# 48 drains on TensorE behind the loop of a decode kernel, and a load of x that waits for SyncE

## The chip, the core and the metric

The kernel runs on one core of one Trainium2 chip. The metric is the device time of one execution in microseconds; the span is the time from the first to the last instruction in the profile of one execution, and is a little shorter than the execution's own time.

## What is computed

One decode step (one new token for each of four sequences): a layer norm, then attention over the last 4096 positions of a cache and a SwiGLU feed-forward network side by side, both added to the input.

```python
# B=4, D=512, Hq=32, Hkv=8, Sk=16384, Dh=128, W=4096, F=1792, bfloat16
xn = layernorm(x)
q = xn @ wq                                    # [4, 32 heads, 128]
k, v = k_cache[:, :, Sk - W:], v_cache[:, :, Sk - W:]     # each kv head serves 4 q heads
p = softmax(q @ k.T * Dh ** -0.5)
attn = (p @ v) @ wo
ffn = (silu(xn @ w_gate) * (xn @ w_up)) @ w_down
out = x + attn + ffn
```

## The kernel before

The kernel is written engine by engine, with semaphores between the engines set by hand. The order of each engine's work is the order in the text; there is no scheduler.

**The work and its loop.** The 4 x 8 pairs of sequence and kv head are taken two at a time: 16 steps `d`, each with a K block and a V block of 2 MB (two sequences x 4096 positions x 128). K and V have two buffers each in SBUF. TensorE runs a loop of 8 rounds (line 425) with two steps `b` in each. A step waits for its K block, then takes, in this order: `transposes(0)` (the first half of K, against an identity matrix, into four PSUM banks), `max_rows` (the transposed row maxima of the step before), `pv(b, 1)` (the second half of probabilities times V of an earlier step), `scores(0)`, `shift` (subtracts the row maximum by a small matrix product into the score bank), `transposes(1)`, `pv(1 - b, 0)`, and `scores(1)`. VectorE copies the transposed K out of PSUM (L294), reduces the row maxima (L299), and divides by the denominators (L310 to L314). ScalarE does the exponentials (L263).

**SyncE** issues nearly all loads from one queue, in this order: WQ (4 MB, L231), K(0), K(1) (L217), the gate and up weights WG and WU (L234, L235), V(0) (L221), then in turn K(d) and V(d - 1), each behind a wait until TensorE has released the buffer: `s_tr` for K, `s_pv` for V. Behind those come WD (L240), the last V block in two halves (L225), which wait for the sixteenth increment of `s_pv`, and WO in four pieces (L229). `s_pv` is incremented by `pv(b, 1)`, which stands inside the loop.

**ScalarE** issues the load of x (4 KB, L252) as its first instruction. VectorE waits for x, reduces its sum (L272), and ScalarE and VectorE go in turn through the layer norm (L254, L256, L274, L258, L276, L260). TensorE transposes the result (L359), VectorE copies it to `XnT` (L279), and TensorE then waits for WQ and forms the 32 products of the Q projection.

**Behind the loop** TensorE has, in order: the last `max_rows`, which waits for VectorE's reduction `s_rm`, `pv(0, 1)`, the last `shift`, the gate and up products, the residual x, the two halves of the last `pv`, the down products (L354 with `wd_sb`), four transposes of the attention output (L462), four products that put the heads in order, and 64 products with WO, in pieces of 32, 20, 8 and 4, each behind the wait for its piece of WO:

```python
            for c in range(NO):
                if c in WO_CUTS:
                    eng.wait_ge(d_wo[WO_CUTS.index(c)], 16)
                for n in range(2):
                    last = mm(ps_acc[64 * n:64 * n + B, 0:256], OP[:, c, :], WO[:, c, 256 * n:256 * n + 256])
```

All of down products, residual and WO products add up in one PSUM bank (`ps_acc`), which VectorE copies out at the end (L349), and SyncE and ScalarE store half each.

## Time and profile before

| | |
|---|---|
| median of 3 runs | 197.38 us (197.1 to 198.93) |
| the profiled execution | 196.99 us |
| its span | 195.2 us |
| mean granted clock of TensorE | 0.991 |
| busy: TensorE, VectorE, ScalarE, GpSimd | 160.9, 114.8, 16.6, 10.3 us |
| moved by DMA | 81.10 MB, mean 416 GB/s over the span |
| share of the chain that ended last | DMA 63%, TensorE 32% |

A row of the timeline has start, duration, engine, line, operation, output and inputs, the number of merged instructions, and in brackets the idle time before it with what ended it. `PEld` is TensorE's weight load, `SPq`, `ACTq` and `PEldq` are sequencers: instructions that the engine itself does not execute, such as the issue of a DMA, a drain or a branch. A row of the windows view has a stretch, its length, the busy time of each engine with its instructions, the granted clock, the share of the DMA engines and GB/s. Line 354 is the helper `mm`, through which most products go; there the names of the tiles tell them apart.

### The profile page before, as it was taken

The page shows a single profiled execution, that of the slowest core. Times are in us where ns is not written, and L with a number is a line of the kernel's source. Part 1 is how long each engine was busy: PE and PEld are TensorE (multiplying, and loading weights), DVE is VectorE, ACT ScalarE, POOL GpSimd, SP SyncE. Part 2 cuts the span into 40 slices and gives each one's busy share as a digit, 9 for nine tenths or more (in the row PEclk, how much of TensorE's full clock was granted, in tenths as well). Part 3 has the DMA queues.
Part 4 walks back from the last instruction along what each step waited for, and adds up shares of the span by engine and source line. Part 5 has one row for each costly group of instructions (what it writes and reads, how often), then busy time and mean ns, then how long its engine had stood idle before and what let it go on. Part 6 is the DMA issues. An engine that isn't in the chain of part 4 may idle for free.

```text
span 195.2 us, 7741 instructions
## 1 busy us (share of the span) xinstructions
PE 160.9 (82%) x3458; PEld 139.5 (71%) x3458; DVE 114.8 (59%) x250; ACT 16.6 (9%) x26; POOL 10.3 (5%) x23
## 2 busy tenths in 40 slices
PE   0127999379898989898989898989898989898954
PEld 0113898368887888788878887878787878786742
DVE  1004777337676767676767676767676767675610
ACT  6600101001010101010101010101010101010100
POOL 8930000000000000000000000000000000000000
PEclk9999999879999999999999999999999999999999
DMA  6999999999999999999999999999999999999991
GB/s 216 430 430 433 435 423 428 425 433 433 430 437 430 430 433 430 430 437 430 433 430 433 430 430 433 430 430 430 430 433 430 430 430 433 430 431 417 442 404 64
DMA packets 5934, 81.10 MB, mean 416 GB/s; under 512 B 668, under 2 KB 680, under 8 KB 936
## 3 DMA queue, kind: packets, MB, share of 16 engines
q1 hardware_dynamic: 5912, 81.01, 97.5%
q8 instruction: 5, 0.08, 0.1%
q10 hardware_dynamic: 16, 0.01, 0.0%
q14 instruction: 1, 0.01, 0.0%
HBM read 81.01 MB, written 0.00 MB: 415 GB/s over the span
## 4 chain that ended last, share of the span: by engine, by line
DMA 63%; PE 32%; issue 1%; DVE 1%; SPq 1%; DVEq 0%
DMA kbuf<-in_A_k_cache_dram 48%; PE ps_kt L382 16%; DMA wo_sb<-in_A_wo_dram 9%; PE ps_s L354 8%; DMA wq_sb<-in_A_wq_dram 6%; PE ps_o L354 5%; PE ps_kt L354 2%; PE ps_acc L354 2%; DVE kT L294 1%; SPq L225 1%; DVE kT L282 0%; SPq L229 0%; DVE y_sb L349 0%; DVE qz L285 0%; DVEq L293 0%
## 5 line engine op out<-in xcount | busy, mean ns | idle before, releaser
L294 DVE COPY kT<-ps_kt 128x1024 bf16<-128x1024 bf16 x128 | 79.5, 684 | 25.3 <-PE ps_kt L382 25.3
L382 PE MATMUL ps_kt<-ident,kbuf 128*128 128x128 bf16 x1024 | 62.8, 219 | 10.6 <-DMA kbuf<-in_A_k_cache_dram 10.6
L382 PEld LDWEIGHTS ps_kt<-ident,kbuf 128*128 128x128 bf16 x1024 | 57.3, 98 | 15.8 <-issue 15.7
L354 PE MATMUL ps_o<-p,vbuf 128*128 128x64 bf16 x1120 | 39.0, 194 | 0.0
L354 PEld LDWEIGHTS ps_s<-qz,kT 128*128 128x128 bf16 x1024 | 32.1, 99 | 6.7 <-issue 3.6
L354 PEld LDWEIGHTS ps_o<-p,vbuf 128*128 128x128 bf16 x1120 | 35.8, 99 | 1.1
L354 PE MATMUL ps_s<-qz,kT 128*128 x1024 | 35.3, 193 | 1.2
L299 DVE TENSOR_REDUCE rm<-ps_s 128x8 bf16<-128x512 f32 x17 | 11.8, 692 | 23.5 <-PE ps_s L354 23.5
L263 ACT ACTIVATE p<-ps_s 128x512 bf16<-128x512 f32 x17 | 10.1, 597 | 162.4 <-PE ps_s L354 162.4
L354 PE MATMUL ps_o<-p,ones 128*128 128x128 bf16 (+1 forms) x69 | 6.9, 220 | 4.4 <-DMA vbuf<-in_A_v_cache_dram 3.0
L354 PEld LDWEIGHTS ps_o<-p,ones 128*128 128x128 bf16 x69 | 4.5, 98 | 5.5 <-DMA vbuf<-in_A_v_cache_dram 3.2
L354 PE MATMUL ps_kt<-wq_sb,xnT 128*32 128x512 bf16 x32 | 3.6, 629 | 5.6 <-DMA wq_sb<-in_A_wq_dram 5.6
L354 PE MATMUL ps_s<-dg,ones 8*128 8x512 bf16 x17 | 6.5, 385 | 0.0
L354 PE MATMUL ps_s<-mkc,mkr 2*128 2x512 bf16 x17 | 6.5, 385 | 0.0
L359 PE MATMUL ps_acc<-i,xn 4*128 4x4 f32 x4 | 0.6, 254 | 7.1 <-ACT xn L260 7.1
L354 PEld LDWEIGHTS ps_kt<-wq_sb,xnT 128*32 128x32 bf16 x32 | 1.2, 137 | 7.2 <-issue 7.2
L282 DVE STREAM_TRANSPOSE kT<-ps_kt 128x512 f32<-128x512 f32 x2 | 1.4, 716 | 8.3 <-PE ps_kt L354 8.3
L354 PE MATMUL ps_acc<-wo_sb,oP 128*4 128x256 bf16 x64 | 4.1, 272 | 1.8 <-DMA wo_sb<-in_A_wo_dram 1.8
L359 PEld LDWEIGHTS ps_acc<-i,xn 4*128 4x128 f32 x4 | 0.6, 207 | 7.1 <-issue 7.1
L310 DVE TENSOR_REDUCE den<-ps_o 128x8 f32<-128x128 f32 x18 | 4.9, 274 | 1.0 <-PE ps_o L354 1.0
L207 POOL MEMSET vbuf<- 128x6144 f32 x1 | 5.2, 5222 | 0.0
L354 PEld LDWEIGHTS ps_acc<-wo_sb,oP 128*4 128x4 bf16 x64 | 2.5, 84 | 3.3 <-DMA wo_sb<-in_A_wo_dram 1.9
(65 smaller groups left out, 48.0 us busy)
## 6 DMA issues: line engine op xcount, KB each, us to landing
kbuf<-in_A_k_cache_dram SPq DMA_DIRECT2D x16, 2048.0 KB, 12.6
vbuf<-in_A_v_cache_dram SPq DMA_DIRECT2D x15, 2048.0 KB, 11.3
wq_sb<-in_A_wq_dram SPq DMA_DIRECT2D x1, 4096.0 KB, 12.4
vbuf<-in_A_v_cache_dram SPq DMA_DIRECT2D x2, 1024.0 KB, 9.2
wo_sb<-in_A_wo_dram SPq DMA_DIRECT2D x1, 2048.0 KB, 14.4
wg_sb<-in_B_w_gate_dram SPq DMA_DIRECT2D x1, 1792.0 KB, 25.8
wu_sb<-in_B_w_up_dram SPq DMA_DIRECT2D x1, 1792.0 KB, 29.4
wd_sb<-in_B_w_down_dram SPq DMA_DIRECT2D x1, 1792.0 KB, 15.0
```

What stands on the lines that cost most here:

```text
L207: eng.memset(VB[:, HKN:].bitcast(FP32), 0.0)
L225: eng.dma_start(VB[:, a:a + HKN], kv_ap(A_v_cache, d)[:, :, h * HKN:(h + 1) * HKN]).then_inc(done, 16)
L263: eng.activation(P[:, d % 2 * PS:d % 2 * PS + SN], ps_S[d % 2][:], ACT.Exp, scale=SCALE).then_inc(s_p, 1)
L282: eng.transpose(qT[:, 512 * n:512 * n + 512], ps_kt[n][:])
L294: eng.tensor_copy(KT[:, u * HKN + 1024 * g:u * HKN + 1024 * (g + 1)], kt_ps[g].rearrange("p a b -> p (a b)")).then_inc(s_ev, 1)
L299: eng.tensor_reduce(RM[:], ps_S[bank][:].rearrange("p (t c) -> p c t", c=C), AX.X, ALU.max).then_inc(s_rm, 1)
L310: eng.tensor_reduce(den[:], den_ps.rearrange("p (t c) -> p c t", c=C), AX.X, ALU.add)
L354: return eng.matmul(o, l, r, start=start, stop=stop, skip_group_check=True)
L359: last = eng.transpose(xT_ps[:, c * B:(c + 1) * B], xn[:].rearrange("b (p c) -> b c p", c=NC)[:, c, :], I4[:])
L382: last = eng.transpose(kt_ps[g][:, k, :], KB[:, a:a + 128], ident[:])
```

## The change

Two edits. Behind TensorE's loop, ahead of the last `max_rows`, stand 48 drain instructions, each of which lets the sequencer go on when the engine has finished what it was given. And ScalarE's load of x, the first instruction of that engine, waits for a new semaphore `s_go`, which SyncE increments with a `nop` right behind its issue of K(1).

```diff
+    s_go = sem("s_go")
...
             eng.dma_start(WQ[:], wq_ap).then_inc(d_wq, 16)
             load_k(0)
             load_k(1)
+            eng.nop().then_inc(s_go, 1)
             eng.dma_start(WG[:], wg_ap).then_inc(d_wg, 16)
             eng.dma_start(WU[:], wu_ap).then_inc(d_wu, 16)
...
         @block.scalar
         def _(eng):
+            eng.wait_ge(s_go, 1)
             eng.dma_start(X[:], x_ap).then_inc(d_x, 16)
...
                     scores(1, ev + NG, b, q)
+
+            for _ in range(48):
+                eng.drain()
             max_rows(ND + 1)
             pv(0, 1, ND + 1)
             shift(1, ND + 1)
```

## The prediction

> **What bounds the kernel now.** I read the page's summary first, then the chain that ended last, then the timelines of the two places that are edited (the first 16 us and the last 20 us).

> ```profile
> span 195.2 us, 7741 instructions
> ...
> GB/s 216 430 430 433 435 423 428 425 433 433 430 437 430 430 433 430 430 437 430 433 430 433 430 430 433 430 430 430 430 433 430 430 430 433 430 431 417 442 404 64
> ```

> From the second slice to the last but one the DMA engines move some 430 GB/s without a break: the loads stream through and the compute engines follow. The end of the chain shows what finishes the kernel:

> ```profile
> 171.95 0.54 SPq L225
> ...
> 173.83 16.82 DMA wo_sb<-in_A_wo_dram
> ...
> 190.69 2.23 PE ps_acc L354 x32
> ...
> 192.95 0.43 DVE y_sb L349
> ```

> The last loads (two halves of V, four pieces of WO) are issued from 171.95 on, when the loop's last `pv` is done; both edits leave that step inside the loop. TensorE ends at 192.92, VectorE copies, the store goes out. So a delay of TensorE behind the loop costs nothing until its own chain ends later than the last piece of WO allows. How much room that is decides this case.

> **Edit 1: the 48 drains.** They stand between the last `scores` of the loop and `max_rows(ND + 1)`.

> ```profile
> 176.73 1.06 PE L354 MATMUL ps_s<-qz,kT 128*128 x32
> 177.83 0.69 DVE L299 TENSOR_REDUCE rm<-ps_s 128x8 bf16<-128x512 f32 x1 [1.15 <-PE ps_s L354]
> 178.57 0.22 PE L354 MATMUL ps_acc<-ident,rm 128*8 128x128 bf16 x1 [0.78 <-DVE rm L299]
> ...
> 186.08 0.41 DVE L345 COPY oB<-ps_kt 32x512 bf16<-32x512 bf16 x1 [1.03 <-PE ps_kt L462]
> 186.54 0.22 PEld L354 LDWEIGHTS ps_kt<-oB,rep 32*128 32x128 bf16 x4 [0.68 <-DVE oB L345]
> 186.98 0.44 DVE L347 CAST oP<-ps_kt 128x128 bf16<-128x128 f32 x1 [0.49 <-PE ps_kt L354]
> 187.68 1.91 PE L354 MATMUL ps_acc<-wo_sb,oP 128*4 128x256 bf16 x32 [0.74 <-DMA wo_sb<-in_A_wo_dram]
> 190.69 2.22 PE L354 MATMUL ps_acc<-wo_sb,oP 128*4 128x256 bf16 x32 [1.09 <-DMA wo_sb<-in_A_wo_dram]
> ```

> There are two covers. The first is the 0.78 us in which TensorE waits for the row maxima anyway (177.79 to 178.57). The second is the wait for WO at the end. The 32 first products take 1.91 us, so one costs (1.91 - 0.27)/31 = 0.053 us and all 64 without a wait 63 x 0.053 + 0.27 = 3.6 us. VectorE has `OP` ready at 187.42; a step from VectorE to TensorE takes 0.05 us (186.49 to 186.54). Free of the DMA, TensorE would end at 187.47 + 3.6 = 191.1, and it ends at 192.92: 1.8 us of room. (WO itself is in by 192.5: the last issue at 174.8 and 17.7 us, rows below, so at 191.1 + 1.8 its wait is over too.) Between the two covers nothing absorbs: TensorE is busy all the time, and waits for no load there that a later start could find landed:

> ```profile
> 180.00:182.00 2.00, 2.00 (x37) 0.94 (x36) 1.35 (x5) 0.84 (x2) 0.00 (x0) 1.00 1.08 459
> 182.00:184.00 2.00, 2.00 (x67) 2.00 (x68) 1.49 (x5) 0.01 (x1) 0.00 (x0) 1.00 1.03 430
> ```

> Now the price of one drain behind another, which this trace does not hold. What it holds:

> ```profile
> L491 PEldq DRAIN  x1: 8/8/8, 0.3 to 0.3; - x1
> L425 PEldq ALU_OP  x1: 32/32/32, 177.2 to 177.2; - x1
> L425 PEldq COMPARE_BRANCH  x1: 76/76/76, 177.3 to 177.3; - x1
> 172.31 0.27 DVE L310 TENSOR_REDUCE den<-ps_o 128x8 f32<-128x128 f32 x1
> 172.66 0.20 DVE L312 RECIPROCAL den<-den 128x8 f32<-128x8 f32 x1
> L229 SPq DMA_DIRECT2D wo_sb<-in_A_wo_dram x4: 432/432/601, 173.2 to 174.8; - x4
> 173.18 2.02 SPq L229 DMA_DIRECT2D wo_sb<-in_A_wo_dram  x4
> wo_sb<-in_A_wo_dram SPq DMA_DIRECT2D x1, 256.0 KB, 17.7
> ```

> TensorE's one drain with nothing to wait for executes in 8 ns. An instruction of the sequencer costs more than its execution, though: SyncE's four issues execute in 601 + 3 x 432 = 1897 ns and take 2.02 us, so 41 ns pass between two. On TensorE's own sequencer the loop's addition (32 ns) and its branch start about 0.1 us apart, which leaves some 0.07 us between. VectorE has a drain between its reduction and its reciprocal, and 0.08 us between the end of the one (172.58) and the start of the other. Bounds for one drain in a row: 0.008 + 0.041 = 0.049 us below, 0.1 us above (the spacing of TensorE's pair). I take 0.08 us: TensorE's own pair with the first one's 32 ns replaced by 8 gives 0.076, VectorE's row 0.08. The first drain also waits until the products are done, so the row starts at 177.8.

> 48 x 0.08 = 3.84 us. TensorE restarts at 177.79 + 3.84 + 0.05 = 181.68 in place of 178.57: 3.1 us late. 1.8 us of that vanish in the wait for WO; 1.3 us are exposed. At 0.049 us a drain: 2.35 us, 1.6 us late, all hidden. At 0.1: 4.8 us, 4.1 us late, 2.3 exposed.

> [...]

> **What the idle time does to the clock.** The drains keep the array idle for 3.9 us. The trace has one idle stretch of that kind, 3.03 us in front of 37.50:

> ```profile
> 37.50 0.40 PE L354 MATMUL ps_o<-p,ones 128*128 128x128 bf16 x4 [3.03 <-DMA vbuf<-in_A_v_cache_dram]
> 37.73 1.71 PE L354 MATMUL ps_o<-p,vbuf 128*128 128x64 bf16 x32
> 44.46 1.11 PE L354 MATMUL ps_o<-p,vbuf 128*128 128x64 bf16 x32
> 37.50:39.20 1.70, 1.70 (x35) 1.70 (x36) 0.00 (x0) 0.00 (x0) 0.00 (x0) 0.64 0.99 414
> 39.20:41.00 1.80, 1.79 (x37) 1.70 (x34) 0.00 (x0) 0.00 (x0) 0.00 (x0) 0.50 0.98 419
> 41.00:42.40 1.40, 0.00 (x0) 0.00 (x0) 0.69 (x1) 0.00 (x0) 0.00 (x0) 0.87 1.01 433
> 190.00:192.00 2.00, 1.31 (x22) 0.87 (x24) 0.00 (x0) 0.00 (x0) 0.00 (x0) 1.00 0.53 205
> ```

> The third figure from the end is the granted clock. It falls to a half soon after the wait and is back by 42.4: at a half for 1.7 x 0.72 + 1.8 + 1.4 x 0.26 = 3.4 us. The same 32 products then take 1.71 us in place of 1.11, so 35% of that time is lost where TensorE is the bound. An idle 1.09 us (the last row) left the clock alone. 3.9 us are longer than the 3.03 that made it fall, so I expect it to fall here, right where TensorE has no idle time: up to 3.4 x 0.35 = 1.2 us, and since part of the low stretch can lie in the stall itself, I take 1.1 us. Bounds: 0 and 1.2.

> [...]

> **Edit 2: x waits for SyncE.**

> ```profile
> 0.81 0.56 ACTq L252 DMA_DIRECT2D x_sb<-in_A_x_dram  x1
> 1.27 1.29 SPq L217 DMA_DIRECT2D kbuf<-in_A_k_cache_dram  x2
> 2.27 0.67 DVE L272 TENSOR_REDUCE st_neg<-x_sb 4x1 f32<-4x512 bf16 x1 [2.27 <-DMA x_sb<-in_A_x_dram]
> 7.73 0.17 DVE L279 CAST xnT<-ps_acc 128x16 bf16<-128x16 f32 x1 [1.55 <-PE ps_acc L359]
> 13.30 3.18 PE L354 MATMUL ps_kt<-wq_sb,xnT 128*32 128x512 bf16 x28 [5.61 <-DMA wq_sb<-in_A_wq_dram]
> 21.93 0.55 SPq L221 DMA_DIRECT2D vbuf<-in_A_v_cache_dram  x1
> ```

> The issue of x moves from 0.81 behind SyncE's second K, 2.56: 1.75 us later, and the whole normalisation on ScalarE, VectorE and TensorE (with ScalarE's table loads, which stand behind the waiting load) moves with it. x landed 1.46 us after its issue; the chain from there to `XnT` takes 7.90 - 2.27 = 5.63 us; the Q projection waits for WQ until 13.2. So x may land as late as 7.5 us, 4.9 us after the new issue. From below it lands as fast as before, at 4.0. From above it stands behind all 8 MB already queued: 8.39 MB at 430 GB/s are 19.5 us, so about 21.3. Which is nearer? A packet of code went through while SyncE's queue held far more than that:

> ```profile
> 3.24 0.45 SPq L235 DMA_DIRECT2D wu_sb<-in_B_w_up_dram  x1
> wu_sb<-in_B_w_up_dram SPq DMA_DIRECT2D x1, 1792.0 KB, 29.4
> q8 instruction: 1, 0.02, 5.4%
> ```

> The last row is of the DMA view from 23.8 to 24.9 us, while WU (issued at 3.24, 29.4 us to landing) is not in before 32.6. Another queue's packet takes its turn among SyncE's. x is four rows on ScalarE's own queue, so I expect it by 5 to 7 us: cost nothing, hidden by WQ. Even an x that comes with WQ at 13.2 only moves the projection by 5.6 us and the load of V(0) to 27.5, with the DMA queue busy until 32.6. Without the cover the upper bound decides: the projection 13.6 us late, V(0) issued at 35.5 in place of 21.93, the queue dry from 32.6 for 2.9 us and the start of a transfer (1.5 us by x's row): +4.4 us. SyncE's `nop` costs a few hundredths in front of loads that queue behind 8 MB: nothing.

> **Sum.** The profiled execution took 196.99 us (span 195.2 and 1.8 around it; 0.2% below the median of the runs shown, 197.38). 196.99 + 1.3 (drains past both covers) + 1.1 (clock) + 0 (x) = 199.4 us.

> **Rivals.**
> - Not slower: the drains fit. At 0.049 us a drain or less the delay is at most 1.6 us, ends inside the wait for WO, and the idle 2.4 us are shorter than any that lowered the clock: 197.0. It decides below 2.6/48 = 0.054 us. For it: the 8 ns row. Against it: no row shows TensorE's sequencer passing two instructions of its own in under 0.1 us. Chance 0.20.
> - [...] Chance 0.15.
> - Dear drains: 0.1 us each, 2.3 us exposed, with the low clock's 1.2 at its full: 200.5. For it: TensorE's pair. Chance 0.17.
> - x stands behind the bulk: 196.99 + 4.4 = 201.4, or more with the drains. The code packet speaks against it. Chance 0.05.

> **How the numbers follow.** The forecast, drains past both covers and the clock down, has 0.41; 0.02 is left for faster, for which I know no mechanism (the stream of the DMA is untouched). The range goes from the hidden case, 196.9, to the dear one with a little more, 201.0. One per cent, 2 us, is about what a measurement of this kernel tells from no change. Slower by more: most of the forecast (0.36), the dear drains (0.17), x (0.05) and a little of the clock's rival (0.02): 0.60. Within it: 0.20 + 0.13 + 0.05 = 0.38. Faster 0.02.

> **What the profile after would show.** The first `max_rows` behind the loop at 181.7 (step one; at 180.2 the drains are cheap, at 182.7 dear). The first WO products at about 191 to 192 and all 64 without a wait, VectorE's last copy at about 195.3. PEclk at 5 to 8 in the slices behind 181. The last WO piece still landing at 192.5. x landing before 7.5 and the Q projection still at 13.3, released by WQ. I am wrong if TensorE still waits for WO at the end, if the Q projection starts late and V(0)'s load with it, or if the loop's loads move at all.

## The result and the profile after

The changed kernel takes 199.54 us (median of 6 runs, 199.32 to 200.49) against 197.29 us before (6 runs): a ratio of 1.0107, 95% interval 1.0067 to 1.0147. The forecast was 199.4 us. The profiled execution took 199.32 us with a span of 197.6 us, 2.3 and 2.4 us more than before.

The page's first parts (TensorE's clock and the DMA rate in 40 slices, then the shares of the chain that ended last):

```profile
span 197.6 us, 7790 instructions
...
PEclk9999999859999999999999999999999999999799
...
GB/s 219 432 425 428 431 424 435 433 425 428 401 425 438 428 441 434 431 428 425 428 438 425 441 434 431 428 425 428 438 431 434 434 431 428 420 426 438 422 306 2
...
DMA 49%; PE 40%; issue 4%; DVE 3%; ACT 2%; SPq 1%; DVEq 0%; ACTq 0%
```

The stream of loads is about as full as before until the last two slices. What is new stands at the end: the clock falls to 7 tenths in the third slice from the end, and the last slice (192.7 to 197.6 us) holds no transfers to speak of: the loads are in, and TensorE still works. The timeline behind the loop:

```profile
176.74 1.06 PE L357 MATMUL ps_s<-qz,kT 128*128 x32
177.84 0.69 DVE L302 TENSOR_REDUCE rm<-ps_s 128x8 bf16<-128x512 f32 x1 [1.16 <-PE ps_s L357]
181.22 0.22 PE L357 MATMUL ps_acc<-ident,rm 128*8 128x128 bf16 x1 [3.41 <-issue]
181.37 1.57 PE L357 MATMUL ps_o<-p,vbuf 128*128 128x64 bf16 x32
183.40 1.68 PE L357 MATMUL ps_kt<-wg_sb,xnT 128*32 128x448 bf16 x16
...
191.66 3.66 PE L357 MATMUL ps_acc<-wo_sb,oP 128*4 128x256 bf16 x64 [0.53 <-DVE oP L350]
195.36 0.42 DVE L352 CAST y_sb<-ps_acc 128x256 bf16<-128x256 f32 x1 [3.75 <-PE ps_acc L357]
```

The loop ends where it ended before (its last scores from 176.74, before 176.73). `max_rows` follows at 181.22, 2.65 us late; what it waited for is now "issue", the sequencer. The 64 WO products run in one piece, released by VectorE, and end at 195.32 in place of 192.91. The drains by their line:

```profile
L444 PEldq DRAIN  x48: 8/8/437, 177.4 to 181.2; - x48
```

The first drain waits 437 ns for the products, to 177.85. The others execute in 8 ns (the median of the row), and yet the last one starts at about 181.15, just ahead of `max_rows`: (181.15 - 177.85)/47 = 0.07 us from one to the next, nearly all of it between them. The windows view of the same stretch and of what follows (the third figure from the end is the granted clock):

```profile
178.00:181.20 3.20, 0.00 (x0) 0.00 (x0) 0.53 (x1) 0.00 (x0) 0.00 (x0) 1.00 1.03 438
181.20:183.40 2.20, 2.18 (x35) 1.59 (x35) 0.85 (x4) 0.00 (x0) 0.00 (x0) 0.64 1.03 439
183.40:185.20 1.80, 1.80 (x21) 0.76 (x24) 0.37 (x3) 0.60 (x1) 0.00 (x0) 0.50 1.01 428
185.20:187.20 2.00, 2.00 (x51) 1.39 (x44) 1.69 (x4) 0.25 (x1) 0.00 (x0) 1.00 0.97 408
```

The clock falls to a half within the first microsecond after TensorE restarts: a mean of 0.64 over 2.2 us is 1.6 us at a half and 0.6 us before them (in the same view, 1.00 from 181.2 to 181.8 and 0.50 from 181.8 to 185.2).

The start of the kernel, where x is loaded:

```profile
2.67 0.55 ACTq L255 DMA_DIRECT2D x_sb<-in_A_x_dram  x1
8.30 0.67 DVE L275 TENSOR_REDUCE st_neg<-x_sb 4x1 f32<-4x512 bf16 x1 [8.30 <-DMA x_sb<-in_A_x_dram]
13.99 0.62 PE L357 MATMUL ps_kt<-wq_sb,xnT 128*32 128x512 bf16 x3 [0.27 <-DVE xnT L282]
22.63 0.55 SPq L222 DMA_DIRECT2D vbuf<-in_A_v_cache_dram  x1
```

x lands at 8.3, 5.6 us behind its issue, and no longer in time: the Q projection starts at 13.99, released by `XnT` and not by WQ, and V(0)'s load goes out at 22.63 in place of 21.93. Up to the loop's end nothing is left of this.

### The profile page after: what moved, and what is told of

Read it like the earlier page. It is cut to its first block, busy times and chain, and to the rows that moved or that the text cites. A ratio compares the mean times of both kernels' runs of the same rounds, so it can differ in the third digit from the quotient of the medians.

```text
span 197.6 us, 7790 instructions
## 1 busy us (share of the span) xinstructions
PE 162.8 (82%) x3458; PEld 141.1 (71%) x3458; DVE 115.0 (58%) x250; ACT 16.6 (8%) x26; POOL 10.3 (5%) x23
## 4 chain that ended last, share of the span: by engine, by line
DMA 49%; PE 40%; issue 4%; DVE 3%; ACT 2%; SPq 1%; DVEq 0%; ACTq 0%
DMA kbuf<-in_A_k_cache_dram 46%; PE ps_kt L385 17%; PE ps_s L357 9%; PE ps_o L357 7%; PE ps_acc L357 4%; PE ps_kt L357 3%; DMA x_sb<-in_A_x_dram 3%; DVE kT L297 1%; ACT L261 1%; SPq L218 1%; ACT xn L263 0%; ACT xsq L259 0%; ACT xc L257 0%; DVE kT L285 0%; DVE rm L302 0%
## 5 line engine op out<-in xcount | busy, mean ns | idle before, releaser
L385 PE MATMUL ps_kt<-ident,kbuf 128*128 128x128 bf16 x1024 | 64.2, 222 | 9.8 <-DMA kbuf<-in_A_k_cache_dram 9.8
L385 PEld LDWEIGHTS ps_kt<-ident,kbuf 128*128 128x128 bf16 x1024 | 58.6, 99 | 15.0 <-issue 15.0
L357 PE MATMUL ps_acc<-ident,rm 128*8 128x128 bf16 x17 | 3.7, 219 | 3.4 <-issue 3.4
L307 DVE TENSOR_REDUCE m<-ps_acc 8x1 f32<-8x128 f32 x17 | 4.6, 270 | 2.9 <-PE ps_acc L357 2.9
L275 DVE TENSOR_REDUCE st_neg<-x_sb 4x1 f32<-4x512 bf16 x1 | 0.7, 674 | 8.3 <-DMA x_sb<-in_A_x_dram 8.3
L357 PEld LDWEIGHTS ps_acc<-ident,rm 128*8 128x8 bf16 x17 | 1.4, 82 | 5.2 <-issue 3.5
L317 DVE TENSOR_TENSOR oT<-ps_o,den 128x8 f32 (+1 forms) x18 | 3.0, 167 | 2.9 <-issue 2.7
## 6 DMA issues: line engine op xcount, KB each, us to landing
wg_sb<-in_B_w_gate_dram SPq DMA_DIRECT2D x1, 1792.0 KB, 25.7
wu_sb<-in_B_w_up_dram SPq DMA_DIRECT2D x1, 1792.0 KB, 29.4
wd_sb<-in_B_w_down_dram SPq DMA_DIRECT2D x1, 1792.0 KB, 15.0
```

What stands on the lines that cost most here:

```text
L307: eng.tensor_reduce(m8[:], mt_ps, AX.X, ALU.max)
L317: eng.tensor_tensor(OT[:, 2 * b:2 * b + 2, ds(r * REP, REP)], O_ps.rearrange("p (j h) -> p j h", j=2), den[:].rearrange("p (j h) -> p j h" ...
L357: return eng.matmul(o, l, r, start=start, stop=stop, skip_group_check=True)
L385: last = eng.transpose(kt_ps[g][:, k, :], KB[:, a:a + 128], ident[:])
```

## The experiments

Theory A: of the 2.4 us some 0.9 are drains past both covers, 1.5 are the low clock, and x costs nothing. Rivals: x has a share by way of a WO that lands later (193.3 in this profile, before 192.5), called Theory B below; the covers are smaller than worked out; the clock is not a price of its own.

**Each edit alone.** Drains without the waiting load:

```diff
-            eng.nop().then_inc(s_go, 1)
...
-            eng.wait_ge(s_go, 1)
```

> The 48 drains alone; x is loaded as before. Theory A (drains 0.84 us past both covers, 1.5 us of low clock, x free): +2.3 to 2.5 us over before, the drains 68 ns apart, the first max_rows behind the loop at 181.2, x landed by 2.3. Theory B (the late x gives about 0.8 us of it, by way of WO landing later): +1.5 to 1.7 us, WO in by 192.5 again.

Measured: 1.0141 of before, 1.0117 to 1.0164 (medians 200.25 and 197.21 us). x alone:

```diff
-            for _ in range(48):
-                eng.drain()
```

> The late x alone; no drains. Theory A: the same time as before within 0.3 us; x lands near 8.3, the Q projection starts 0.7 us late at 14.0, V(0)'s load with it, and WO's last piece at 192.5 as before. Theory B: WO's last piece lands near 193.3 and the kernel takes 0.8 us longer.

Measured: 1.0011 of before, 0.9990 to 1.0033. So x is free as far as these runs can tell (0.7 us at most), and the drains are the loss. Theory B falls: the last piece of WO was in by about 192.7 in the profiles of both runs. Why it came later with both edits is not shown; the WO products did not wait for it. But the drains alone cost 2.8 us (2.3 to 3.2), more than Theory A's 2.3 to 2.5. The windows of their profile show why, here cut in lengths of 3.4 us, as long as the clock was down in the changed kernel:

```profile
176.10:179.50 3.40, 1.54 (x49) 1.33 (x45) 1.20 (x2) 0.00 (x0) 0.00 (x0) 1.00 1.01 426
179.50:182.90 3.40, 1.76 (x31) 1.65 (x32) 0.50 (x2) 0.00 (x0) 0.00 (x0) 0.50 1.06 451
182.90:186.30 3.40, 3.40 (x40) 1.38 (x37) 1.31 (x4) 0.78 (x2) 0.00 (x0) 0.50 0.97 411
```

In this execution the clock fell at 179.5, while the drains still ran, and came back at 186.3: 6.8 us of low clock in place of 3.4. `max_rows` starts at 181.14, much as in the changed kernel, but the WO products at 192.36 and not at 191.66:

```profile
181.14 0.27 PE L354 MATMUL ps_acc<-ident,rm 128*8 128x128 bf16 x1 [3.41 <-issue]
192.36 3.66 PE L354 MATMUL ps_acc<-wo_sb,oP 128*4 128x256 bf16 x64 [0.54 <-DVE oP L347]
```

That is 0.7 us, as are the two profiled executions' times apart (199.32 and 200.04). `max_rows` is 2.57 us late here, so the low clock cost 192.36 - (187.47 + 2.57) = 2.3 us. The other runs of the two kernels lie between 199.3 and 200.5 us; whether they differ by the same cause was not profiled.

The profile of x alone shows how near the start came to its limit. Here the expectation missed: x landed at 9.04 in place of 8.3, and V(0)'s load did not follow at 22.6.

```profile
9.04 0.67 DVE L275 TENSOR_REDUCE st_neg<-x_sb 4x1 f32<-4x512 bf16 x1 [9.04 <-DMA x_sb<-in_A_x_dram]
14.72 3.61 PE L357 MATMUL ps_kt<-wq_sb,xnT 128*32 128x512 bf16 x32 [0.27 <-DVE xnT L282]
20.50 3.59 PE L385 MATMUL ps_kt<-ident,kbuf 128*128 128x128 bf16 x32
26.14 0.55 SPq L222 DMA_DIRECT2D vbuf<-in_A_v_cache_dram  x1
```

The first 32 transposes take 3.59 us, before 1.96, and so V(0)'s load went out at 26.14, 4.2 us late, though the Q projection was only 1.4 us late. Why these products were slow is not shown: the windows view has the granted clock at 1.00 there.

```profile
20.00:24.00 4.00, 4.00 (x34) 3.39 (x33) 2.77 (x4) 0.00 (x0) 0.00 (x0) 1.00 1.00 428
```

It cost nothing that the runs show, and SyncE's queue was not empty before 32.9 (WU's landing).

**The stall without the idle array.** Products into an unused PSUM bank in the place of the drains, 60 for the same length of stall:

```diff
-            for _ in range(48):
-                eng.drain()
+            for _ in range(60):
+                mm(ps_kt[2][:, 0:128], ident[:], ident[:], start=True)
```

> 60 products of 128x128 by 128x128 into an unused PSUM bank in the place of the 48 drains, x as before: TensorE is late by about the same 2.6 to 2.8 us, but not idle. They add nothing to the output. Theory A: the clock stays at 1.00 behind 181 and the kernel is 0.8 to 1.1 us over before. Rival (the low clock is not a price of its own, the restart is): +2.4 us as with the drains.

Measured: 1.0021 of before, 1.0007 to 1.0034 (197.71 us). From its timeline:

```profile
177.71 3.51 PE L354 MATMUL ps_kt<-ident 128*128 128x128 bf16 x60
181.15 0.22 PE L354 MATMUL ps_acc<-ident,rm 128*8 128x128 bf16 x1
190.05 3.66 PE L354 MATMUL ps_acc<-wo_sb,oP 128*4 128x256 bf16 x64 [0.53 <-DVE oP L347]
```

and a stretch behind the stall in the windows view:

```profile
181.00:183.00 2.00, 2.00 (x46) 1.44 (x47) 0.98 (x4) 0.23 (x1) 0.00 (x0) 1.00 0.98 410
```

`max_rows` is as late as with the drains (181.15), the clock stays at 1.00, the WO products start at 190.05, which is 187.47 + 2.58, and the profiled execution ends 0.8 us later than before. The runs give less, 0.4 us (0.1 to 0.7). With the same lateness and no idle time most of the loss is gone: 0.4 of 2.8 us are left by the runs, 0.8 of 3.1 by the spans of the profiles. So the low clock is a price of its own, and the larger one, once the lateness has used up the room.

**Shorter stalls.** 24 drains, and 30 products with about the same lateness:

> 24 drains, x as before. Theory A: 177.85 + 24 x 0.068 = 179.5, so max_rows starts 0.95 us late, inside the 1.8 us of room, and the idle 1.75 us leave the clock alone: the same time as before within 0.2 us. Rival (no room behind the first cover; each late us counts): +0.9 us.

> 30 products into an unused bank in the place of the drains, x as before; they add nothing to the output. max_rows at 179.45, 0.9 us late, as with 24 drains, but TensorE busy. Theory A (0.9 us fit into the 1.8 us of room; what 24 drains cost was the clock): the time of before within 0.2 us, clock 1.00. Rival (the room is smaller than 1.8 us): +0.4 to 0.6 us as with 24 drains.

Measured: 1.0020 (1.0006 to 1.0033) with 24 drains, 1.0004 (0.9981 to 1.0028) with 30 products. The timeline with 24 drains:

```profile
179.63 0.22 PE L354 MATMUL ps_acc<-ident,rm 128*8 128x128 bf16 x1 [1.71 <-DVE rm L299]
190.13 3.66 PE L354 MATMUL ps_acc<-wo_sb,oP 128*4 128x256 bf16 x64 [0.53 <-DVE oP L347]
```

the windows view of the same execution, in lengths of 3.4 us:

```profile
177.40:180.80 3.40, 1.69 (x53) 1.49 (x48) 1.19 (x3) 0.00 (x0) 0.00 (x0) 1.00 1.03 436
180.80:184.20 3.40, 3.40 (x36) 1.18 (x33) 1.31 (x4) 0.84 (x2) 0.00 (x0) 0.50 1.02 431
```

and the timeline with 30 products:

```profile
179.43 0.22 PE L354 MATMUL ps_acc<-ident,rm 128*8 128x128 bf16 x1
188.33 1.91 PE L354 MATMUL ps_acc<-wo_sb,oP 128*4 128x256 bf16 x32 [0.53 <-DVE oP L347]
190.80 2.20 PE L354 MATMUL ps_acc<-wo_sb,oP 128*4 128x256 bf16 x32 [0.56 <-DMA wo_sb<-in_A_wo_dram]
```

The 30 products make TensorE 0.86 us late and it still waits for WO at 190.80: hidden, as Theory A said, as far as the interval tells; the room is there. The 24 drains make it 1.06 us late (the profile names VectorE's reduction as what ended the wait, but that was done at 178.64; the drains came last), which would be hidden too, but the clock fell: the WO products start at 190.13, 1.6 us later than 187.47 + 1.06, and 0.2% are lost. Here Theory A was wrong on when the clock falls: an idle 1.7 us was followed by the fall, where it had said that it leaves the clock alone.

**More and fewer drains.**

> 96 drains, x as before. Theory A: restart at 177.85 + 96 x 0.0683 + 0.05 = 184.45, 5.9 us late; 1.8 hidden, 4.1 exposed, and 1.5 to 2.3 us of low clock: +5.6 to 6.4 us. Rival (the sequencer's spacing is not constant, code has to be fetched): more than 7 us.

> 8 drains, x as before: 177.85 + 8 x 0.068 + 0.05 = 178.45, ahead of the row maxima at 178.52. Theory A: max_rows still at 178.57 released by VectorE, and the time of before within 0.2 us. Rival (the first cover does not hide drains, since the sequencer no longer runs ahead): max_rows 0.1 to 0.4 us late, though the end stays with WO.

Measured: 1.0293 (1.0254 to 1.0332; 203.38 us) with 96, 1.0003 (0.9981 to 1.0026) with 8. The row of the 96 drains:

```profile
L440 PEldq DRAIN  x96: 8/8/437, 177.2 to 184.6; - x96
```

what follows them in the timeline:

```profile
184.63 0.26 PE L354 MATMUL ps_acc<-ident,rm 128*8 128x128 bf16 x1 [7.07 <-issue]
```

and the same place with 8:

```profile
178.16 0.69 DVE L299 TENSOR_REDUCE rm<-ps_s 128x8 bf16<-128x512 f32 x1 [1.16 <-PE ps_s L354]
178.90 0.22 PE L354 MATMUL ps_acc<-ident,rm 128*8 128x128 bf16 x1 [0.78 <-DVE rm L299]
```

The median with 96 is 6.2 us over before, and the ratio gives 5.8 (5.6 to 6.4 were expected). The profiled execution, at 204.06 us the slowest of the four, is 7.1 us over that of before; in its windows view the clock is at a half from 180.9 to 191.2, 6.5 us of that behind the restart. The mean spacing is (184.6 - 177.6)/95 = 0.073 us, hardly more than with 48, so the rival of a spacing that grows falls. Eight stay ahead of the row maxima: the wait is 0.78 us and VectorE's, to the figure that of before. The first cover hides drains.

**How late x may come, and what its lateness depends on.** x behind the second K in SyncE's own queue (the edit below), and, in two runs more without drains, the waiting load of ScalarE released after WQ alone and after WU (the `nop` moved up or down):

```diff
-            eng.dma_start(X[:], x_ap).then_inc(d_x, 16)     # ScalarE
...
             load_k(1)
+            eng.dma_start(X[:], x_ap).then_inc(d_x, 16)     # SyncE
```

> x is issued by SyncE behind K(1), in SyncE's own queue; no drains. Theory A (x free as long as V(0)'s load is issued before SyncE's queue runs dry at 32.6): x lands near 22 behind WQ, K(0) and K(1), the Q projection starts near 28, V(0) is issued at 37 to 41, the DMA rate falls to nearly nothing for 5 to 9 us around 33 to 40, and the kernel takes 4.5 to 9 us longer. Rival (the late start is made up in the loop, where TensorE has 0.7 us to spare a step): at most 1 us longer.

> x waits until SyncE has issued WQ alone (the nop moved up); no drains. x is issued near 1.3. Theory A (x takes its turn among packets in flight, however much is queued): it lands 5 to 6.5 us behind its issue, near 7, at or just inside the 7.5 us that WQ covers, and the Q projection starts at 13.3. Rival (the backlog counts): with WQ alone ahead it lands within 3.5 us of its issue.

> x waits until SyncE has issued the up weights (the nop moved down behind WU); no drains. x is issued near 3.8. Theory A (turns): it lands 5 to 6.5 us later, 9 to 10.5, the Q projection starts at 14.7 to 16.2, and the time is that of before within 0.5 us. Rival (backlog): another 3.7 MB are queued ahead, x lands 8 us later still, near 18.

x in SyncE's queue: 1.0430 of before, 1.0390 to 1.0469 (206.1 us). The DMA rate on its page, in slices of 5.1 us:

```profile
GB/s 250 462 381 442 418 407 0 183 407 410 428 423 420 446 423 433 439 414 446 423 439 433 414 449 423 442 426 417 449 420 442 426 423 446 417 437 419 426 414 52
```

and two rows of its timeline:

```profile
22.79 0.67 DVE L272 TENSOR_REDUCE st_neg<-x_sb 4x1 f32<-4x512 bf16 x1 [22.79 <-DMA x_sb<-in_A_x_dram]
37.11 0.55 SPq L221 DMA_DIRECT2D vbuf<-in_A_v_cache_dram  x1
```

x lands behind the 8 MB ahead of it, V(0) goes out at 37.1, and from about 31 to 38 the stream stands still. The kernel is 8.9 us slower, so the loop makes up nothing of that: the rival falls. With ScalarE's queue, released after WQ:

```profile
1.29 0.55 ACTq L255 DMA_DIRECT2D x_sb<-in_A_x_dram  x1
8.05 0.67 DVE L275 TENSOR_REDUCE st_neg<-x_sb 4x1 f32<-4x512 bf16 x1 [8.05 <-DMA x_sb<-in_A_x_dram]
```

and after WU:

```profile
3.79 0.55 ACTq L255 DMA_DIRECT2D x_sb<-in_A_x_dram  x1
10.12 0.68 DVE L275 TENSOR_REDUCE st_neg<-x_sb 4x1 f32<-4x512 bf16 x1 [10.12 <-DMA x_sb<-in_A_x_dram]
```

6.8 and 6.3 us from issue to use, against 5.6 and 6.4 in the two kernels that wait for the second K. Behind WQ alone it is not sooner, behind 3.7 MB more not later: in these four executions the backlog does not count. In the changed kernel x's packets went through among those of SyncE's loads: its DMA view has none of x's queue (q10) from 2.67 to 6 us, and from 6 to 8 us eight of them beside 31 of SyncE's (q1). The first figure is over the 5 to 6.5 us expected, and there the Q projection started at 13.74 and not at 13.3; after WU it started at 15.81, as expected. (Each of the two was run once, 198.24 and 197.18 us against 196.92 before; nothing is read from these times.)

## Why the prediction was right, step by step

- What bounds the end, and the 1.8 us of room in the wait for WO: right. 30 products, 0.86 us late, cost nothing that the runs show; 60 cost in the profile the 0.8 us that are over (0.4 in the runs).
- The price of a drain: 0.07 us measured (0.08 predicted, 0.049 to 0.1 as bounds). The nearest row, TensorE's own pair of sequencer instructions, was the right one, a little too dear. So 2.65 us late in place of 3.1, and 0.87 us exposed in place of 1.3.
- The rival by which the drains fit, with the 8 ns row for it: the execution is 8 ns in the median of the rows of drains here too, but the spacing decides (0.07 us, over the 0.054 us below which the rival would have held), and the rival falls.
- The clock: the fall was right and the term too small. It fell behind the stall and stayed down for 3.4 us; that cost 191.66 - (187.47 + 2.65) = 1.54 us in place of 1.1, over the upper bound of 1.2 too. The step that failed is the share lost, 35% from one group of products, where 1.54/3.4 = 45% were lost. That group, from 37.73, began before the clock fell: by the prediction's own row (0.72 of the 1.7 us from 37.50 at a half) it fell at 37.98, so a part of the group ran at full speed and the share came out too small. That the clock could be down for 6.8 us, as with the drains alone, was not foreseen. When it falls was off as well: I took an idle time of 3 us as the case known to lower it, and with 24 drains it fell behind 1.7 us.
- x: free, as forecast, but not for the reason given. The prediction had it land in 5 to 7 us on the clock of the span, ahead of 7.5; it landed at 8.3 and 9.0, so WQ did not hide it whole. The prediction allowed some 2.4 to 4.4 us from issue to use, with no row for the size; 5.6 and 6.4 were measured. So a sign that it had named for being wrong came true, the Q projection and V(0)'s load starting late, and only its price was nothing. What hid it is the second cover that the prediction named, SyncE's queue, full until 32.6. With x behind 8 MB the price was 8.9 us, where the upper bound was worked out as 4.4: the queue ran dry as said, but V(0) went out 1.6 us later than reckoned, and WU was in at 31.3 (issued at 3.58, 27.7 us to landing) and not at 32.6; the last 1.6 us were not taken apart. SyncE's `nop`, priced at a few hundredths of a microsecond, came with WG's issue at 2.71 in place of 2.60.
- The two misses in size (0.4 us too much for drains, 0.4 too little for the clock) cancel by luck, so the sum of 2.4 us is closer than its terms.

## What to carry to other kernels

Price a sequencer instruction by the spacing of two of its kind on the same engine, never by its own duration: here 8 ns against 70. When TensorE is made to stand still, look at what its clock does afterwards: two thirds of this loss (1.54 of 2.4 us by the profiles) came from work that was slow after the stall, not from the stall. And the lateness of a load was free here as long as the queue that it holds up still had work; the time at which that queue runs dry is the figure to know.

## What the runs showed of the hardware

```profile
184.70:188.10 3.40, 2.15 (x38) 1.59 (x34) 1.12 (x4) 0.00 (x0) 0.00 (x0) 1.00 0.97 414
```

  No limit follows from this, neither in busy nor in idle time. Near the start of the execution with 30 products a stretch with 2.36 us of products, whose longest idle gap is 1.05 us, was followed by half the clock, and one with 1.40 us, in an idle gap of 2.90 us, was not:

```profile
30.26:33.67 3.41, 2.36 (x49) 1.62 (x46) 1.35 (x6) 0.60 (x1) 0.00 (x0) 1.00 0.96 406
33.67:37.09 3.42, 3.03 (x28) 2.76 (x28) 2.43 (x4) 0.00 (x0) 0.00 (x0) 0.50 1.03 441
40.50:43.91 3.41, 1.40 (x25) 1.41 (x26) 0.74 (x2) 0.00 (x0) 0.00 (x0) 1.00 1.00 428
43.91:47.30 3.39, 3.39 (x79) 2.66 (x76) 2.70 (x8) 0.00 (x0) 0.00 (x0) 1.00 1.05 449
```

  Where the stretches of half the clock lie against the kernel differs: the clock fell at 181.8 and at 179.5 in two executions with the same 48 drains. What decides whether it falls stays open.
- A load of 4 KB on ScalarE's queue took 1.46 us from issue to use when it was issued together with SyncE's first bulk load, and 5.6 to 6.8 us when it was issued later beside these loads, whatever was queued there (4, 8 or 12 MB).
